# Second half's x and the MLP's h turned by VectorE's 32x32 blocks instead of by TensorE

## The chip, the cores and the metric

One core of one Trainium2 chip runs the whole program. The metric is device time in microseconds (us) of one execution, as the median of several runs; a profiled execution of the same program gives the trace from which the durations below come. The engines are named as the profile names them: PE (TensorE matmuls), PEld (its weight loads), DVE (VectorE), ACT (ScalarE), POOL (GpSimd) and SP (SyncE, which here only issues transfers).

## What is computed

One transformer block over 2048 tokens of 1024 features: a layer norm, an attention of 32 heads with a learned feature map and no quadratic part, a residual, a second layer norm, a ReLU MLP of width 3584, and a second residual.

```python
def _A_ref(x, wqkv, w_phi, wo):            # attention; H = 32, Dh = 32
    q, k, v = ...                          # x @ wqkv, by heads
    pq = einsum("bhsd,hdf->bhsf", q, w_phi);  pk = einsum("bhsd,hdf->bhsf", k, w_phi)
    phi_q = concat([softmax(pq), softmax(-pq)]);  phi_k = concat([softmax(pk), softmax(-pk)])
    kv = einsum("bhsf,bhsd->bhfd", phi_k, v);  z = phi_k summed over s
    o = einsum("bhqf,bhfd->bhqd", phi_q, kv) / (einsum("bhqf,bhf->bhq", phi_q, z) + 1e-6)
    return o @ wo
def _B_ref(x, w1, w2):
    return einsum("bsf,fd->bsd", maximum(einsum("bsd,df->bsf", x, w1), 0), w2)
h  = x + _A_ref(_layernorm(x), A_wqkv, A_w_phi, A_wo)
h2 = h + _B_ref(_layernorm(h), B_w1, B_w2)
```

## The kernel before, in words

Every product of two float32 matrices is made of three matmuls (`mm3`, L181 to L183): each operand is split into a high part and a low part of a shorter type, and high-high, high-low and low-high are added up in PSUM. A group of three such matmuls, each with 512 moving columns, is one **step**. The program is written as a list of items of 8 steps (4 in the MLP), and all other work is hung on steps by hand: `when(step, f, ...)` puts the call `f` into the program behind that step, `do(n, k, f, ...)` behind step k of item n. Each engine runs its own instructions in the order in which they were written, and semaphores do the rest. So a step number is a place in the order, not a time.

The items come in this order. Tokens stand in 16 tiles of 128, in two halves of 8 tiles.

1. For each half: keys and values (`kv_item`, 4 slabs of heads over 8 tiles), then queries (`q_item`, 2 slabs over 8 tiles). The stationary operand is `xT[t]`, the normalized x of a tile with features on the partitions, high and low part.
2. Projection by `wo` (`wo_item`, 4 groups of 4 tiles, 2 halves of the features, 32 tile-halves in all). Between these items PE makes the attention's numerators (`at_num`, L678), in 16 pairs of units, from blocks that DVE has turned (`at_turn`, L664) and POOL has scaled.
3. The MLP up (`up_item`) and down (`down_item`), by a seven-product scheme (Strassen and Winograd's) on halves of tokens and features: the operands 1 to 7 are sums and differences of quarter blocks. The moving operand of an up step is `hT[m]`, the stationary one a piece of w1. Two blocks of 8 tiles follow each other, `b` = 0 and 1.

**Turning x.** `ln_load` loads a tile of x with tokens on the partitions, `ln_norm` (L243, ACT) normalizes it, and `ln_turn` (L250) turns it: 4 PE transposes of 128x128 into one PSUM bank, twice per tile. `split` (L177 and L178) then takes the high part with ACT and the low part with DVE from that bank. The tiles of the second half are turned while the queries' last slab of the first half is projected; their statistics were made much earlier (`scx`).

**Turning h.** `wo_add` (L728) adds x to the projection's bank, `wo_store` writes the sum to `hd[t]` in DRAM. `ln_pair(b, i, stage)` takes two tiles, 4 apart: loads them (stage 0), makes statistics with DVE (1, L220) and POOL (2, L229 to L231), normalizes (3, L243), turns them on PE (4 to 7, L250 and L758) with an ACT copy out of each bank (L252 and L759), and forms the sums that the scheme wants (L760 and L761 on DVE, L766 and L767 on POOL). `ln_store` writes the seven operands to `hs[b, m]`; `h_load` brings them back, `h_high` (L792) and `h_low` (L796) split them into `hT[m]`. Block 0's pairs lie in the wo items, block 1's in the up items of block 0. The table LN2 has the steps of the stages.

**Weights.** `Units` loads weight pieces in the order of their use into 6 raw buffers, splits them (ACT L124, then POOL or DVE L128) into a ring of 10, and runs ahead of PE as far as these allow. All these loads, the loads of x and h and the stores go through SP's one queue, in written order; the attention's blocks (`ed`) go through ACT's queue.

**The end.** `d_load` brings h back from `hd`, `d_add` (L886) adds the MLP's banks to it, `d_store` writes the output.

## Time and profile before

| | us |
|---|---|
| median of 3 runs | 1881.68 (1880.31 to 1882.74) |
| the profiled execution, whole | 1881.49 |
| its span, first to last instruction | 1879.7 |
| PE busy | 1872.6 |
| DVE busy | 1063.6 |
| POOL busy | 976.9 |
| ACT busy | 741.0 |

The span is what the trace shows; the whole execution is 1.8 us longer. Matmuls overlap in the pipeline, so PE's time is read from the distance between the starts of its instructions, not from their durations. In a timeline row the columns are the start in us from the span's start, the duration, engine, line, operation, what is written and read, the shape and the count; in a row of groups there are the busy time, the mean of one in ns and, behind the second bar, the idle time ahead of it and what ended that.

### The profile page before, as it was taken

The numbers are of one execution on the slowest core, as the hardware profiler recorded it, in microseconds if no ns is written. First come the engines' busy times: TensorE is split into PE (matmuls) and PEld (weight loads), VectorE is DVE, ScalarE is ACT, GpSimd is POOL, SyncE is SP. The second block draws the span as 40 slices with busy tenths as digits, with TensorE's granted clock in tenths as the row PEclk, the third lists the DMA queues.
The fourth block names the chain that finished last, engine by engine and source line by source line (L and its number), as shares of the span: only waits on it lengthen the run. The fifth ranks groups of instructions, "written<-read, shape, count | busy, mean of one in ns | idle before, by whom it ended". The sixth has DMA issues, their size and how long they took to land.

```text
span 1879.7 us, 31869 instructions
## 1 busy us (share of the span) xinstructions
PE 1872.6 (100%) x11630; PEld 1540.3 (82%) x11630; DVE 1063.6 (57%) x1714; ACT 741.0 (39%) x1264; POOL 976.9 (52%) x956
## 2 busy tenths in 40 slices
PE   9999999999999999999999999999999999999999
PEld 7888888888888888888888888888888888888887
DVE  7788688677789777455444664444433333343333
ACT  5322244222233122355455554444444444444442
POOL 3778733677745988223343234445444444444443
PEclk9999999999999999999999999999999999999999
DMA  6889875454475567886877997877877677777775
GB/s 214 268 280 312 269 262 180 148 155 141 140 232 190 203 216 237 264 254 209 263 233 241 312 297 248 264 246 259 275 239 216 201 230 239 237 213 220 216 215 177
DMA packets 293036, 433.21 MB, mean 230 GB/s; under 512 B 24208, under 2 KB 150160, under 8 KB 292880
## 3 DMA queue, kind: packets, MB, share of 16 engines
q1 hardware_dynamic: 263712, 390.26, 65.3%
q10 hardware_dynamic: 29168, 40.93, 6.5%
q8 instruction: 91, 1.49, 0.3%
q14 instruction: 65, 0.53, 0.1%
HBM read 293.73 MB, written 137.36 MB: 229 GB/s over the span
## 4 chain that ended last, share of the span: by engine, by line
PE 98%; DVE 1%; ACT 0%; POOL 0%; DMA 0%; issue 0%; SPq 0%; DVEq 0%; POOLq 0%
PE mm L181 25%; PE mm L182 25%; PE mm L183 25%; PE ac L181 4%; PE ac L182 4%; PE ac L183 4%; PE tp L182 2%; PE tp L181 2%; PE tp L183 2%; PE tp L250 1%; PE tp L678 1%; PE ac L491 1%; PE ac L678 1%; PE tp L297 0%; DVE st L220 0%; PE tp L758 0%
## 5 line engine op out<-in xcount | busy, mean ns | idle before, releaser
L128 POOL TENSOR_TENSOR w<-raw,w 128x512 fp32r<-128x512 f32 x353 | 474.6, 1347 | 671.5 <-ACT w L124 638.0
L124 ACT ACTIVATE w<-raw 128x512 fp32r<-128x512 f32 x686 | 409.1, 626 | 491.8 <-PE mm L183 238.9
L128 DVE TENSOR_TENSOR w<-raw,w 128x512 fp32r<-128x512 f32 x333 | 275.0, 827 | 512.9 <-ACT w L124 507.3
L181 PE MATMUL mm<-w,xT 128*128 128x512 f32 x752 | 299.4, 398 | 0.0
L183 PE MATMUL mm<-w,xT 128*128 128x512 f32 x752 | 293.1, 390 | 0.0
L182 PE MATMUL mm<-w,xT 128*128 128x512 f32 x752 | 293.0, 390 | 0.0
L181 PE MATMUL mm<-hT,w 128*128 128x512 f32 x672 | 262.6, 391 | 0.0
L183 PE MATMUL mm<-hT,w 128*128 128x512 f32 x672 | 261.6, 389 | 0.0
L182 PE MATMUL mm<-hT,w 128*128 128x512 f32 x672 | 261.5, 389 | 0.0
L378 POOL TENSOR_TENSOR b<-b 128x256 f32<-128x256 f32 x168 | 129.0, 769 | 85.2 <-DMA b<-in_w_dram 75.4
L181 PEld LDWEIGHTS mm<-w,xT 128*128 128x128 f32 x752 | 141.2, 188 | 31.4 <-issue 2.2
L183 PEld LDWEIGHTS mm<-w,xT 128*128 128x128 f32 x752 | 141.2, 188 | 30.0
L182 PEld LDWEIGHTS mm<-w,xT 128*128 128x128 f32 x752 | 141.3, 188 | 28.5 <-issue 1.0
L181 PE MATMUL mm<-w 128*128 128x512 f32 x392 | 152.5, 389 | 0.0
L182 PE MATMUL mm<-w 128*128 128x512 f32 x392 | 152.5, 389 | 0.0
L183 PE MATMUL mm<-w 128*128 128x512 f32 x392 | 152.5, 389 | 0.0
L183 PEld LDWEIGHTS mm<-hT,w 128*128 128x128 f32 x672 | 126.1, 188 | 26.5
L181 PEld LDWEIGHTS mm<-hT,w 128*128 128x128 f32 x672 | 126.2, 188 | 25.8
L182 PEld LDWEIGHTS mm<-hT,w 128*128 128x128 f32 x672 | 126.2, 188 | 25.7
L480 POOL TENSOR_TENSOR zacc<-zacc,kphi 128x512 f32<-128x512 f32 x60 | 83.8, 1397 | 14.3 <-DVE kphi L472 14.3
L181 PEld LDWEIGHTS mm<-w 128*128 128x128 f32 x392 | 73.6, 188 | 15.3
L182 PEld LDWEIGHTS mm<-w 128*128 128x128 f32 x392 | 73.6, 188 | 15.3
(173 smaller groups left out, 3183.1 us busy)
## 6 DMA issues: line engine op xcount, KB each, us to landing
raw<-t SPq DMA_DIRECT2D x224, 256.0 KB, 4.0
raw<-ad SPq DMA_DIRECT2D x196, 256.0 KB, 3.0
raw<-in_w_dram SPq DMA_DIRECT2D x168, 256.0 KB, 3.2
ad<-c SPq DMA_DIRECT2D x112, 256.0 KB, 4.2
b<-in_w_dram SPq DMA_DIRECT2D x42, 512.0 KB, 5.7
t<-b SPq DMA_DIRECT2D x42, 512.0 KB, 3.6
ad<-s SPq DMA_DIRECT2D x84, 256.0 KB, 4.6
ed<-qe ACTq DMA_DIRECT2D x32, 512.0 KB, 3.9
```

Of the source, the lines that this page charges most:

```text
L124: nc.scalar.activation(w[:, 0, :], raw[1], AF.Copy)
L128: eng.tensor_tensor(out=w[:, 1, :], in0=raw[1], in1=w[:, 0, :].bitcast(F32), op=ALU.subtract)
L181: pe.matmul(ps, a_hi, b_hi, start=first, stop=False, skip_group_check=more)
L182: pe.matmul(ps, a_hi, b_lo, start=False, stop=False, skip_group_check=more)
L183: pe.matmul(ps, a_lo, b_hi, start=False, stop=last, skip_group_check=more)
L250: pe.transpose(pt[:, k, :], xn[:, (4 * j + k) * P:(4 * j + k + 1) * P], ident)
L378: pool.tensor_tensor(out=tsum[j, *out], in0=tsum[j, *a], in1=tsum[j, *b], op=ALU.subtract)
L480: pool.tensor_tensor(out=zacc[s], in0=zacc[s], in1=phi_of[key], op=ALU.add)
L491: pe.matmul(kv_ps[s][g][32 * i:32 * (i + 1), 0:64], vt[:, 32 * h:32 * (h + 1)], phi[:, 64 * h:64 * (h + 1)], start=first, stop=last)
L678: pe.matmul(banks[g][32 * c:32 * (c + 1), r * P:(r + 1) * P], kvL[rows, 4 * q + 2 * sd + h // 4, 32 * (h % 4):32 * (h % 4 + 1)], phT[rows, ...
```

## The change

The second half's x and all of h are no longer turned on PE. A tile is loaded so that a partition holds a quarter of the features of four tokens, one from each group of 32; DVE then turns the tile in place in 32x32 blocks with one instruction, which leaves features on the partitions.

- **x, second half.** `x_load` loads a tile in 4 transfers, one per group of 32 tokens. Partition 32a+j then holds tokens j of the four groups, features 256a to 256a+255. A scale per token therefore differs between the four column groups, so `x_norm` normalizes with 4 ACT instructions of 256 columns (`turn_norm`), from statistics that `x_stats` has brought into that layout by way of DRAM. `x_turn` is the DVE transpose, `x_high` an ACT copy, `x_low_part` two POOL subtractions. The features come out in another order, so the second half's weights for k, v and q are loaded in that order (`rows_of`).
- **h, sums and statistics.** `wo_add` writes the sum into a new tile `xo` (2 buffers; `xh` goes from 5 to 3) with the features regrouped. `wo_stats` makes the statistics from `xo` at once, `wo_power` finishes them on POOL, `wo_keep` stores two numbers per token.
- **h, turning.** `ln_pair` loads each tile in 4 transfers and the statistics in 4 small ones, normalizes with 4 ACT instructions per tile, and turns each tile with one DVE instruction. The ACT copies are gone. The sums are formed as before. The stage table has other steps.
- **The MLP.** `hT[m]` now holds token groups outermost, so that an up matmul reads its 512 moving columns in 16 runs of 32, 128 columns apart (`h_chunk`). It writes PSUM in plain order (`by_token`). `h_load` is one transfer instead of two.
- **The end.** `d_load` fetches h in the regrouped order into a tile `raw`, and the first `d_add` of an output writes a new tile.

```diff
+    def x_load(t):
+        xin["x", t] = (xlp if t % 4 > 1 else lnp).tile([P, D], F32, name="xl" if t % 4 > 1 else "xin")
+        src = x[t * P:(t + 1) * P, :].rearrange("(g j) (a f) -> g a j f", g=4, a=4)
+        for g in range(4):
+            sp.dma_start(xin["x", t][:, 256 * g:256 * (g + 1)], src[g])
+    def turn_norm(dst, src, scale, bias):
+        for g in range(4):
+            c = slice(256 * g, 256 * (g + 1))
+            act.activation(dst[:, c], src[:, c], AF.Identity, bias=bias(g), scale=scale(g))
+    def x_turn(t):
+        xn = xnt["x", t]
+        v.transpose(xn, xn)
+    def x_high(t):
+        (hi, _), xn = x_parts(t)
+        act.activation(hi, xn, AF.Copy)
+    def x_low_part(t, j):
+        (hi, lo), xn = x_parts(t)
+        k = slice(4 * j, 4 * j + 4)
+        pool.tensor_tensor(out=lo[:, k], in0=xn[:, k], in1=f32(hi[:, k]), op=ALU.subtract)
...
+    def rows_of(w, hf, k):
+        return w[k] if hf == 0 else w.rearrange("(a c) p f -> a (c p) f", a=4)[:, 32 * k:32 * (k + 1), :]
...
     def wo_add(t, hf):
-        v.tensor_add(xh[t, hf], wo_ps.pop((t, hf)), xh[t, hf])
+        v.tensor_add(by_row(xo[t, hf]), by_group(wo_ps.pop((t, hf))), by_group(xh.pop((t, hf))))
+    def wo_stats(t, hf):
+        st = hst[t]
+        v.bn_stats(out=st[:, 6 * hf:6 * hf + 6], in_=xo[t, hf])
+        if hf:
+            v.bn_aggr(out=st[:, 12:14], in_=st[:, 0:12].rearrange("p (j c) -> p j c", j=2))
+    def wo_keep(t):
+        sp.dma_start(shd[t // HT, t % 4][:, t % HT // 4, :], hst.pop(t)[:, 14:16])
...
         if stage == 0:
-            for key in keys:
-                ln_load(key, [hd[key[1]]])
+            for t in tiles:
+                hx[t] = lnp.tile([P, D], F32, name="xin")
+                src = hd[t].rearrange("a (g j) r c -> g a j (r c)", g=4)
+                for g in range(4):
+                    sp.dma_start(hx[t][:, 256 * g:256 * (g + 1)], src[g])
...
-        elif stage in (4, 5, 6):
-            ln_turn(keys[stage // 6], stage != 4)
+        elif stage in (4, 5):
+            ht = hx[tiles[stage - 4]]
+            v.transpose(ht, ht)
...
-            mm3(ps, w[:, 0, cols], w[:, 1, cols], hT[m][:, 0, k, :], hT[m][:, 1, k, :],
+            mm3(by_token(ps), w[:, 0, cols], w[:, 1, cols], h_chunk(m, 0, k), h_chunk(m, 1, k),
+    def h_chunk(m, s, k):
+        return hT[m][:, s].rearrange("p i (g k j) -> p k (i g) j", g=4, k=4)[:, k]
...
+            for step, f, *args in ((-11, x_norm), (-6, x_turn), (0, x_high), (2, x_low_part, 0), (4, x_low_part, 1)):
+                when(turn + step, f, t, *args)
...
-        do(max(n - 2, wo_first), -1, wo_load, t, hf)
+        when(8 * n - 4 if n > wo_first + 1 else wo0, wo_load, t, hf)
...
-    LN2 = ((0, 9, 12, 17, 24, 25, 26, 27, 29, 36), (0, 18, 26, 32, 40, 42, 44, 46, 50, 60))
+    LN2 = ((0, 8, 17, 19, 22, 24, 26, 28, 35), (0, 18, 32, 36, 40, 44, 48, 50, 60))
```

The order of instructions moves on PE, and on the queues around the wo items. On PE, in one wo item of the pair of tiles 1 and 5 (`xin` are the two tiles of h, `tp` the PSUM banks of transposes, `oT` the attention's output), before the change:

```order
L183 MATMUL mm_8359<-w_6311,oT_7774 128x512
L250 MATMUL tp_8368<-ident_398,xin_8050 128x128 x4
L181 MATMUL mm_8359<-w_6342,oT_7774 128x512
L182 MATMUL mm_8359<-w_6342,oT_7774 128x512
L183 MATMUL mm_8359<-w_6342,oT_7774 128x512
L250 MATMUL tp_8378<-ident_398,xin_8050 128x128 x4
L181 MATMUL mm_8359<-w_6835,oT_7774 128x512
```

The same item in the changed kernel:

```order
L183 MATMUL mm_8382<-w_6292,oT_7788 128x512
L181 MATMUL mm_8382<-w_6323,oT_7788 128x512
L182 MATMUL mm_8382<-w_6323,oT_7788 128x512
L183 MATMUL mm_8382<-w_6323,oT_7788 128x512
L181 MATMUL mm_8382<-w_6816,oT_7788 128x512
```

The sets of four transposes are gone and the steps follow each other directly; PE's program has 48 rows of this kind fewer, 16 for x and 32 for h, and is otherwise the same.

On SP's queue, at the load of the same pair (`hd` is h in DRAM, `shd` its statistics, `xh` the residual x, `xo` the new sum), before:

```order
L702 DMA xh_8044<-in_x_dram 128x512
L214 DMA xin_8050<-hd1_85 128x1024
L214 DMA xin_8052<-hd5_89 128x1024
L731 DMA hd2_86<-xh_7790 128x512
L702 DMA xh_8169<-in_x_dram 128x512
```

In the changed kernel:

```order
L824 DMA xin_8054<-hd1_85 128x1x256 x4
L824 DMA xin_8059<-hd5_89 128x1x256 x4
L751 DMA xh_8091<-in_x_dram 128x512
L803 DMA hd2_86<-xo_8002 128x4x128
L812 DMA shd0_2_103<-qmx_7620 128x2
L829 DMA st_8197<-shd0_1_102 32x4x4 x4
L751 DMA xh_8227<-in_x_dram 128x512
```

Where two loads stood ahead of the next residual there are now eight, and a store and four loads of statistics stand between that one and the one after it.

More of the change, by code (lines that the diff above doesn't have):

```diff
@@ L209, in ln_load @@
     def ln_load(key, parts):
-        xin[key] = xlp.tile([P, D], F32, name="xl") if key[0] == "x" and key[1] >= HT and key[1] % 4 > 1 else \
-            lnp.tile([P, D], F32, name="xin")
+        xin[key] = lnp.tile([P, D], F32, name="xin")
         n = D // len(parts)
@@ L240, in ln_norm, with ln_turn @@
     def ln_norm(key):
-        sc, src = xst.pop(("s", key[1]) if key[0] == "x" and key[1] >= HT else key), xin.pop(key)
-        xnt[key] = src if key[0] == "h" else fp_ln.tile([P, D], F32, name="xn")
+        sc, src = xst.pop(key), xin.pop(key)
+        xnt[key] = fp_ln.tile([P, D], F32, name="xn")
         act.activation(xnt[key], src, AF.Identity, bias=sc[:, 1:2], scale=sc[:, 0:1])
-    def ln_turn(key, j, dst=None):
+    def ln_turn(key, j, dst):
         xn = xnt[key]
@@ L974 @@
         do(n, 0, x_open, t)
-        for j in range(2):
+        for j in range(2 if t < HT else 0):
             when(stages[4 + j], ln_turn, ("x", t), j, lambda t=t: xT[t])
```

164 lines of the change are left out of this document (109 added, 55 removed).

## The prediction

> **What bounds the kernel now.** I read the page first, then the chain, then the groups of PE, then PE's timeline.
>
> ```profile
> span 1879.7 us, 31869 instructions
> PE 1872.6 (100%) x11630; PEld 1540.3 (82%) x11630; DVE 1063.6 (57%) x1714; ACT 741.0 (39%) x1264; POOL 976.9 (52%) x956
> PE 98%; DVE 1%; ACT 0%; POOL 0%; DMA 0%; issue 0%; SPq 0%; DVEq 0%; POOLq 0%
> ...
> L250 PE MATMUL tp<-ident,xn 128*128 128x128 f32 x120 | 18.1, 273 | 0.5 <-ACT xn L243 0.4
> L250 PE MATMUL tp<-ident,xin 128*128 128x128 f32 x96 | 14.4, 272 | 0.0
> L758 PE MATMUL tp<-ident,xin 128*128 128x128 f32 x32 | 4.8, 272 | 0.0
> ```
>
> PE is busy all through the span and makes 98% of the chain that ended last, so what leaves PE's program leaves the time, as long as nobody else becomes late. The transposes that go are 64 of the 120 on `xn` (8 tiles of 8) and all 96 + 32 on `xin`: 192, in 48 sets of four. Their durations overlap with their neighbours', so the price of a set is read from starts. PE's timeline in the wo items, around the pair of tiles 1 and 5:
>
> ```profile
> 702.09 0.60 PE L250 MATMUL tp<-ident,xin 128*128 128x128 f32 x4
> 702.45 0.47 PE L181 MATMUL mm<-w,oT 128*128 128x512 f32 x1
> ...
> 703.22 0.60 PE L250 MATMUL tp<-ident,xin 128*128 128x128 f32 x4
> ...
> 707.06 0.40 PE L183 MATMUL mm<-w,oT 128*128 128x512 f32 x1
> ...
> 711.83 0.39 PE L183 MATMUL mm<-w,oT 128*128 128x512 f32 x1
> ...
> 311.70 0.60 PE L250 MATMUL tp<-ident,xn 128*128 128x128 f32 x4
> ...
> 312.38 0.39 PE L182 MATMUL mm<-w,xT 128*128 128x512 f32 x1
> ```
>
> From one set to the next with one step between them it is 1.13 us. A matmul without transposes starts 0.227 us after the last (21 between 707.06 and 711.83), a step therefore takes 0.68, and the set costs 1.13 - 0.68 = 0.45 us. At x it is the same: from the start of the set to the step's second matmul 0.68 us, without the set 0.23, difference 0.45.
>
> **The change, part by part.**
>
> *PE.* 48 sets at 0.45 us: 21.6 us, 7.2 of them at x, 7.2 in the wo items, 7.2 in the first block of up items. Nothing is added to PE's program. Added to its work, perhaps: the 2352 up matmuls now read their columns in 16 runs of 32.
>
> ```profile
> L181 PE MATMUL mm<-hT,w 128*128 128x512 f32 x672 | 262.6, 391 | 0.0
> L181 PE MATMUL ac<-hT,w 128*128 128x512 f32 x112 | 43.9, 392 | 0.0
> L678 PE MATMUL tp<-qe,kvL 32*32 32x128 f32 x896 | 24.8, 278 | 0.0
> L297 PE MATMUL mm<-wt,wphi 32*32 32x256 f32 x224 | 10.4, 386 | 0.0
> ```
>
> (672 + 112) x 3 = 2352. No row shows a large matmul with such an operand. The nearest are L678 and L297, whose moving operands are runs of 32 columns: 278 ns for 4 runs against 272 for 128 plain columns (L250), a difference of 6 ns that may belong to the other shape; 386 for 8 runs, below the 391 of 512 plain columns. The bounds are nothing and 6 ns, 2352 x 6 = 14 us; a gain is excluded, since the columns are as many. I take nothing, because L297 with its 8 breaks shows none. [...]
>
> *DVE.* In the x stage it loses 16 subtractions from PSUM and gains 8 transposes of a whole tile, whose price the attention's turning shows.
>
> ```profile
> L664 DVE STREAM_TRANSPOSE qe<-qe 128x1024 f32<-128x1024 f32 x28 | 34.2, 1227 | 12.1 <-POOL qe L658 9.5 <-POOL qe L648 1.7 <-DMA xh<-in_x_dram 1.0
> L178 DVE TENSOR_TENSOR xT<-tp,xT 128x512 fp32r<-128x512 f32 x30 | 20.3, 678 | 6.1 <-ACT xT L177 6.1
> 262.00:315.00 53.00, 53.00 (x266) 43.80 (x265) 46.28 (x71) 29.18 (x40) 15.12 (x17) 1.00 0.69 227
> ```
>
> 16 x 0.678 = 10.8 go, 8 x 1.227 = 9.8 come. DVE has 46.3 us of work in these 53 (third busy column of the windows' row), and will have 45.3 in 53 - 7.2 = 45.8: full. It may fall a us or two behind there; PE waits for it only when four banks are full, three items of 5.4 us later, and the rest of the keys' stage gives the time back. Nothing is charged. If the backlog grew beyond 16 us it would show one for one.
>
> *ACT and POOL at x.* A normalization in four pieces (8 x 4; 0.38 to 0.82 us each by L453 and L237, I take 0.6) and 8 copies of 1024 (1.06 by L792) replace 8 normalizations (1.24) and 16 copies (0.6 by L177); POOL gets 16 subtractions like L128.
>
> ```profile
> L453 ACT ACTIVATE vt<-mm 128x256 f32<-128x256 f32 x64 | 24.5, 382 | 125.0 <-PE mm L183 125.0
> L237 ACT ACTIVATE xn<-xin,sc 128x512 f32<-128x512 f32 x2 | 1.6, 816 | 2.7 <-POOL sc L231 2.7
> L128 POOL TENSOR_TENSOR w<-raw,w 128x512 fp32r<-128x512 f32 x353 | 474.6, 1347 | 671.5 <-ACT w L124 638.0 <-DMA raw<-t 8.9 <-DVE c L822 5.6
> L792 ACT ACTIVATE hT<-hT 128x1024 fp32r<-128x1024 f32 x28 | 29.6, 1056 | 30.5 <-DMA hT<-hs 29.5 <-DMA raw<-in_w_dram 1.1
> L177 ACT ACTIVATE xT<-tp 128x512 fp32r<-128x512 f32 x30 | 17.9, 597 | 33.2 <-PE tp L250 33.1
> L243 ACT ACTIVATE xin<-xin,sc 128x1024 f32<-128x1024 f32 x16 | 19.3, 1236 | 13.5 <-POOL sc L231 12.7 <-DVE oT L695 0.4
> ```
>
> POOL: 16 x 1.35 = 21.6 more beside the 15.1 in that window. ACT has 29.2 + 32 x 0.6 + 8 x 1.06 - 8 x 1.24 - 16 x 0.6 = 37 us of work in 46. Each tile is wanted seven items after it is turned, 38 us, so this hides behind PE; without that cover a tile's chain, some 8 us, would stand in the open once.
>
> *The wo items.* Here the wait that matters is PE's for the attention's turned blocks. DVE's and PE's timelines at two of the 16 pairs:
>
> ```profile
> 631.11 1.19 DVE L664 STREAM_TRANSPOSE qe<-qe 128x1024 f32<-128x1024 f32 x1
> 632.21 0.34 PE L678 MATMUL tp<-qe,kvL 32*32 32x128 f32 x8
> 645.15 0.34 PE L678 MATMUL tp<-qe,kvL 32*32 32x128 f32 x8
> 651.23 1.25 DVE L664 STREAM_TRANSPOSE qe<-qe 128x1024 f32<-128x1024 f32 x1 [0.66 <-POOL qe L658]
> 658.08 0.34 PE L678 MATMUL tp<-qe,kvL 32*32 32x128 f32 x8
> 640.00:660.00 20.00, 20.00 (x329) 16.02 (x327) 14.05 (x26) 1.36 (x5) 17.09 (x24) 1.00 0.61 204
> ```
>
> At 632 the second block of the pair is ready at 632.30 and used by the second half of the numerators, some 0.8 us after 632.21: 0.7 us to spare. At 658 it is ready at 652.48, 5.6 us ahead. Between 632 and 658 no transpose stands on PE, pairs are 12.9 us apart, and the chain still won 5 us. That is the pace which PE will keep through all the wo items, so the loss of the pauses by itself makes nobody late. What is new in this chain: `wo_stats` puts 0.67 us per tile-half on DVE from the first wo item on (L220), where the statistics used to come later, and `wo_power` puts three POOL instructions per tile ahead of step 132, 8 tiles instead of 4.
>
> ```profile
> L220 DVE BATCH_NORM_STATS2 st<-xin 128x6 f32<-128x512 f32 x64 | 40.6, 674 | 4.8 <-DMA xin<-in_x_dram 2.8 <-DMA xin<-hd 2.0
> 657.57 0.22 POOL L229 TENSOR_SCALAR sc<-mv 128x1 f32<-128x1 f32 x1
> ...
> 658.89 0.22 POOL L229 TENSOR_SCALAR sc<-mv 128x1 f32<-128x1 f32 x1
> ```
>
> Up to the pair at 632 DVE gets 4 x 0.674 = 2.7 us more; a tile's three POOL instructions take 1.3 us (658.89 - 657.57), so POOL gets 4 x 1.3 = 5.3 us more before step 132. DVE and POOL are idle for 6 and 3 us of the 20 above. The loss lies between nothing, if the added work falls into waits, and 2.7 + 5.3 = 8.0 us, if none does. I take 2: the DVE part at the pairs with no reserve, most of it; the POOL part falls on pairs with 5 us. DVE's two h transposes per pair (2.5 us) replace nothing on DVE; they come when pairs have that reserve, or after the attention. `wo_add` now also waits for SP to have stored the `xo` of two halves before, written 11 steps (7.5 us) ahead, against 3.6 us to land:
>
> ```profile
> hd<-xh SPq DMA_DIRECT2D x32, 256.0 KB, 3.6
> xh<-in_x_dram SPq DMA_DIRECT2D x32, 256.0 KB, 4.7
> q1 hardware_dynamic: 263712, 390.26, 65.3%
> ```
>
> Behind it on DVE stand the attention's reductions and turns. SP in turn waits with `wo_keep` for POOL, and the next residual loads stand behind that; a residual is asked for 13 steps (9 us) ahead and lands after 4.7, so SP may be held 4 us before DVE notices, and I add nothing.
>
> *Up and down.* Operand 7 of block 0 is the tightest of the up start: split until 823.53, used at 823.87.
>
> ```profile
> 821.18 2.35 DVE L796 TENSOR_TENSOR hT<-hT 128x1024 fp32r<-128x1024 f32 x2
> ...
> 823.87 0.39 PE L181 MATMUL mm<-hT,w 128*128 128x512 f32 x1
> ```
>
> Its load waits for PE to leave the wo items and so moves with PE; it becomes one transfer in long rows instead of two, a us either way, nothing charged. Block 1's transposes and normalizations have 68 steps of up items per pair instead of 40, and I charge nothing. At the end `d_add` is as many instructions as before.
>
> **The sum**, against the profiled execution's 1881.5 us (the median of the runs shown, 1881.68, is the same within their spread): 1881.5 - 21.6 + 2.0 = 1861.9, so 1862.
>
> **The rivals.**
>
> *The attention's chain takes it back.* The 8.0 us above in full: 1881.5 - 21.6 + 8.0 = 1867.9. For it speaks the 0.7 us at 632, against it the 5 us won by 658. It would show as idle PE ahead of L678.
>
> *The new loads crowd few engines.* The sources of `x_load`, of `ln_pair`'s loads and of `rows_of` have four blocks outermost, where every load before has 128 rows. By the queue's row (packets, MB, share of 16 engines), 65.3% of 16 x 1879.7 us for 390 MB, one engine needs 50 us per MB; a pair of h tiles (1.05 MB) takes 53 us, 3.3 on sixteen engines and 13.2 on four. The 9.9 us more would hold what stands behind them on the queue: a transfer of 256 KB would land after 4.7 + 9.9 = 14.6 us. In the wo items that is 5.6 us beyond the 9 that a residual has, and 5 are the chain's reserve: 1 us per pair. In the up items ACT splits a weight 14 steps (9.5 us) after it was asked for, is held 5 us, and the banks bear 2.7 (one item): 2.3 per pair. Four pairs of each make 13 us, if every wait is paid; I take 9, so 1862 + 9 = 1871. No trace here shows such a load. [...]
>
> *The runs slow the up matmuls: slower than before.* If each of the 15 breaks costs the time of two columns (0.227 us / 512 = 0.44 ns each), a matmul takes 13.3 ns more, 2352 of them 31 us: 1862 + 31 = 1893. It decides from (1881.5 - 1861.9) / 2352 = 8.3 ns, 4% of 227. Against it stands L297.
>
> *The transposes were hidden*, and nothing changes, 1881: the starts at 702 speak against it.
>
> **How the numbers follow.** The forecast 0.58, the chain 0.12, the crowded engines 0.18, the runs 0.10, hidden 0.02. The range runs from 1857.5 (no loss, 1859.9, less the runs' spread and 0.03 us in a set's price) to 1877, which holds the first two rivals unless both come in full (0.03 of the second's 0.18); left out are these, the runs, the hidden case and 0.03 below, 0.18 in all. This kernel's measurement tells 0.2% from no change, 3.8 us. Faster by more: 0.58 + 0.12 + 0.15 = 0.85; within: 0.03 + 0.02 = 0.05; slower: 0.10.
>
> **What would show it.** Right: up matmuls 0.227 us apart, no L250-like rows after the first half's tiles, PE's stages shorter by 7.2 us each, idle PE ahead of the numerators below 3 us. Wrong: starts of up matmuls more than 8 ns further apart; `hd` loads that land 10 us or later; ACT waiting for loads in the up items.

## The result, and the profile after

The changed kernel takes 2008.79 us (median of 5 runs, 2008.51 to 2014.04) against 1880.31 (1880.19 to 1882.74) for the kernel before on the same chip: a ratio of 1.0687, 95% interval 1.0671 to 1.0702. The forecast was 1862 with a range up to 1877; the time lies far outside it, on the other side.

The page of the changed kernel: the span, the busy times, the engines' shares of the chain, and the first row of the up matmuls. The chain could be followed back only to 885 us, so its shares say nothing of the stages before that.

```profile
span 2007.0 us, 31636 instructions
PE 1911.9 (95%) x11438; PEld 1539.6 (77%) x11438; DVE 1075.5 (54%) x1722; ACT 739.5 (37%) x1296; POOL 997.0 (50%) x972
PE 53%; DMA 1%; DVE 1%; SPq 0%; issue 0%; POOL 0%; DVEq 0%; POOLq 0%
...
L181 PE MATMUL mm<-hT,w 128*128 128x512 f32 x672 | 270.5, 402 | 4.5 <-ACT hT L878 2.7
```

PE has 192 instructions fewer and yet 39 us more of busy time, and now it also stands still: 95% busy where it was 100%. The up matmuls are longer, 402 ns where the row showed 391. PE's timeline in the up items of block 1, where nothing waits, gives the distance of their starts:

```profile
1299.61 0.40 PE L181 MATMUL mm<-hT,w 128*128 128x512 f32 x1
1299.84 0.40 PE L182 MATMUL mm<-hT,w 128*128 128x512 f32 x1
1300.08 0.40 PE L183 MATMUL mm<-hT,w 128*128 128x512 f32 x1
1300.31 0.40 PE L181 MATMUL mm<-hT,w 128*128 128x512 f32 x1
```

0.23 to 0.24 us here, 237 ns at the median of all 2352, 227 before. For the rest I cut the span of a profiled execution at PE's starts into stages: the first 40 items, the 8 items in which the second half's x is turned (x stage), the second half's remaining keys and queries, the wo items, the up items of block 0 and of block 1, and the rest. In us:

| kernel | first 40 | x stage | keys, queries | wo | up 0 | up 1 | rest |
|---|---|---|---|---|---|---|---|
| before | 260.1 | 50.3 | 285.7 | 206.1 | 274.1 | 266.3 | 537.2 |
| after | 260.0 | 59.3 | 345.2 | 238.0 | 289.2 | 278.1 | 537.2 |

The loss is 60 us in the second half's keys and queries, a stage that the prediction did not price at all, 32 in the wo items, 9 in the x stage, and 12 to 15 in each block of up items. What PE waited for from the x stage to the end of the queries (us in all, times, longest; before, PE had no such row in that window):

```profile
PE mm L181 <- ACT w L124: 13.9, 1, 13.9
PE mm L182 <- POOL w L128: 12.2, 6, 7.2
PE mm L181 <- DVE qe L612: 10.1, 3, 7.3
PE tp L567 <- POOL zacc L529: 8.9, 2, 5.4
PE mm L182 <- DVE w L128: 6.5, 3, 5.1
```

In the first, second and last row PE lacks the weights' halves, from all three engines that make them; in the other two it waits for work of the attention on DVE and POOL. One step further back stands POOL's wait for `b`, the loads of pieces of w1 and w2 whose sums POOL forms beside the attention. In the kernel before, from 310 to 665 us (us in all, times, longest):

```profile
POOL b L378 <- DMA b<-in_w_dram: 33.9, 10, 5.0
```

In the changed kernel, in the same window:

```profile
POOL b L427 <- DMA b<-in_w_dram: 79.2, 12, 13.4
```

These loads are not touched by the change, and POOL waits up to 13 us for one. They share SP's queue with loads that are new. How few engines the new ones use is seen from 347 to 351 us, where nearly all that moves is the second half's weights, which SP issues one behind the other (PE, PEld, DVE, ACT, POOL busy, then the granted clock, the DMA share and GB/s):

```profile
347.00:351.00 4.00, 4.00 (x20) 3.30 (x19) 0.00 (x0) 0.08 (x1) 1.37 (x2) 1.00 0.27 95
```

A share of 0.27 is 4.3 of the 16 DMA engines, and at 95 GB/s 128 KB take 1.38 us; the mean over the whole span is 216 GB/s.

Of the prediction's own signs of error the first is there: starts of up matmuls 10 ns further apart, where 8 was the bound. So is the third: in the up items ACT waits 14.5 us for loads of weights, 1.1 before. The second, `hd` loads that land late, can't be read, since this trace gives no landing for them.

### The profile page after: what moved, and what is told of

Same layout as the page of the kernel before. It is cut to its first block, busy times and chain, and to the rows that moved or that the text cites. A ratio compares the mean times of both kernels' runs of the same rounds, so it can differ in the third digit from the quotient of the medians.

```text
span 2007.0 us, 31636 instructions
## 1 busy us (share of the span) xinstructions
PE 1911.9 (95%) x11438; PEld 1539.6 (77%) x11438; DVE 1075.5 (54%) x1722; ACT 739.5 (37%) x1296; POOL 997.0 (50%) x972
## 4 chain that ended last, share of the span: by engine, by line
PE 53%; DMA 1%; DVE 1%; SPq 0%; issue 0%; POOL 0%; DVEq 0%; POOLq 0%
PE mm L183 12%; PE mm L181 12%; PE mm L182 12%; PE ac L183 3%; PE ac L181 3%; PE ac L182 3%; PE tp L182 2%; PE tp L181 2%; PE tp L183 2%; DMA hd<-xo 1%; DMA hT<-hs 0%; DVE hT L882 0%; SPq L396 0%; DVE xo L791 0%; DVE w L128 0%
## 5 line engine op out<-in xcount | busy, mean ns | idle before, releaser
L181 PE MATMUL mm<-w,xT 128*128 128x512 f32 x752 | 304.7, 405 | 24.1 <-ACT w L124 13.9
L182 PE MATMUL mm<-w,xT 128*128 128x512 f32 x752 | 300.6, 400 | 18.9 <-POOL w L128 12.2
L183 PE MATMUL mm<-w,xT 128*128 128x512 f32 x752 | 298.4, 397 | 0.0
L181 PE MATMUL mm<-hT,w 128*128 128x512 f32 x672 | 270.5, 402 | 4.5 <-ACT hT L878 2.7
L182 PE MATMUL mm<-hT,w 128*128 128x512 f32 x672 | 269.7, 401 | 3.8 <-DVE hT L882 3.8
L183 PE MATMUL mm<-hT,w 128*128 128x512 f32 x672 | 270.1, 402 | 0.0
L181 PEld LDWEIGHTS mm<-w,xT 128*128 128x128 f32 x752 | 144.8, 193 | 59.7 <-ACT w L124 14.3
L182 PEld LDWEIGHTS mm<-w,xT 128*128 128x128 f32 x752 | 144.8, 193 | 55.0 <-POOL w L128 16.7
L183 PEld LDWEIGHTS mm<-w,xT 128*128 128x128 f32 x752 | 144.7, 192 | 30.5
L513 ACT ACTIVATE ke<-ke 128x512 f32<-128x512 f32 x64 | 40.4, 631 | 144.2 <-DVE ke L509 144.2
L182 PEld LDWEIGHTS mm<-w 128*128 128x128 f32 x392 | 73.6, 188 | 15.3
```

Source lines behind the costliest of these rows:

```text
L181: pe.matmul(ps, a_hi, b_hi, start=first, stop=False, skip_group_check=more)
L182: pe.matmul(ps, a_hi, b_lo, start=False, stop=False, skip_group_check=more)
L183: pe.matmul(ps, a_lo, b_hi, start=False, stop=last, skip_group_check=more)
L513: act.activation(e_of[key], e_of[key], AF.Exp)
```

## The experiments

All ratios are to the kernel before on the same chip, with 95% intervals. There is no kernel 6 or 7. A stage's time is that of the one profiled execution, which can lie a few us beside the median. Kernels 2 to 5, 8, 9, 11, 12, 15 and 16 start from the changed kernel and let columns or feature chunks meet that belong to different tokens or features; kernels 10, 14 and 17 to 20 keep them together.

**1. The runs alone.** The kernel before, with only the operand of the up items read in 16 runs of 32 (tokens in another order):

```diff
...
-            mm3(ps, w[:, 0, cols], w[:, 1, cols], hT[m][:, 0, k, :], hT[m][:, 1, k, :],
+            mm3(by_token(ps), w[:, 0, cols], w[:, 1, cols], h_chunk(m, 0, k), h_chunk(m, 1, k),
```

> The kernel before, whose up matmuls alone now read their 512 columns in 16 runs of 32, 128 columns apart, from the same tiles (so tokens and features are mixed up in the MLP). Theory 'runs' (a broken moving operand costs time by itself): the up matmuls start 0.237 us apart as in the changed kernel, 10 ns more, 2352 x 10 ns = 23.5 us, so 1904 us. Theory 'company' (the 10 ns come from what else runs in the changed kernel): 0.227 us apart and 1880 us.

1903.41 us, ratio 1.0118 (1.0103 to 1.0133). Nothing else moved: up 0 takes 285.5, up 1 278.1 us, all other stages are those of before within 1.6 us. The runs cost 1903.41 - 1880.73 (the kernel before, beside it) = 22.7 us, 9.6 ns for each of 2352 matmuls.

**2 to 4. Plain operands, wide loads, both.** In 3, each load with four blocks outermost gets 32 or 128 rows outermost: x and h in 4 transfers by feature quarter, onto 32 partitions each, instead of by token group, the weights in their plain order. In 2, the operand is read plainly. 4 is both.

```diff
-        src = x[t * P:(t + 1) * P, :].rearrange("(g j) (a f) -> g a j f", g=4, a=4)
-        for g in range(4):
-            sp.dma_start(xin["x", t][:, 256 * g:256 * (g + 1)], src[g])
+        src = x[t * P:(t + 1) * P, :].rearrange("(g j) (a f) -> a j g f", g=4, a=4)
+        for a in range(4):
+            sp.dma_start(xin["x", t][32 * a:32 * (a + 1)].rearrange("p (g f) -> p g f", g=4), src[a])
...
-        return w[k] if hf == 0 else w.rearrange("(a c) p f -> a (c p) f", a=4)[:, 32 * k:32 * (k + 1), :]
+        return w[k]
...
-        return hT[m][:, s].rearrange("p i (g k j) -> p k (i g) j", g=4, k=4)[:, k]
+        return by_token(hT[m][:, s, k, :])
```

> The changed kernel, whose up matmuls read 512 plain columns again (the operand's columns stand in another order, so tokens and features are mixed up in the MLP). Theory 'runs': 0.227 us apart in both blocks of up items, 2009 - 23.5 = 1985 us, and the stretch from 262 to 950 us as it was. Theory 'company': no change, 2009 us.

> The changed kernel with every load made of pieces whose outermost count is 32 or 128: x and h are loaded in 4 transfers by feature quarter onto 32 partitions each, instead of by token group onto 128, and the second half's weights for k, v and q are loaded in plain order (so their features no longer match those of x). Theory 'four engines' (176 transfers with an outermost count of 4 run on 4 of the 16 DMA engines, and PE's stalls and the low clock behind them come from that): the trace shows 16 completions per transfer, no gap of PE above 1 us after the first 62 us but a few, and 1880 - 21.6 + 23.5 + 2 = 1884 us (1880 to 1892). Theory 'work' (the new instructions and waits on DVE, POOL and SP make the stalls): 1985 us or more.

> Both edits: wide loads and plain columns, with the parts of the computation changed that these two change. If the two causes are all there is, what is left is the transposes' 21.6 us and my 2 us of lost reserve: 1861 us (1858 to 1866). If theory 'work' holds, 1960 us or more.

| kernel | us | ratio | x stage | keys, queries | wo | up 0 | up 1 |
|---|---|---|---|---|---|---|---|
| 2 | 1990.46 | 1.0581 (1.0563 to 1.0598) | 62.5 | 342.5 | 234.5 | 285.5 | 266.4 |
| 3 | 1917.58 | 1.0194 (1.0179 to 1.0209) | 43.5 | 301.3 | 213.0 | 285.5 | 278.1 |
| 4 | 1892.87 | 1.0066 (1.0049 to 1.0083) | 43.5 | 302.1 | 211.5 | 270.8 | 266.3 |

The loads cost 2008.8 - 1917.6 = 91 us; the runs, on top of wide loads, 24.7. In 2, plain operands alone win 18.3 us and not 23.5: up 1 is 11.7 us shorter, up 0 only 3.7. That a four-block load runs on four engines only agrees with the smallest packets: the trace of the kernel before has 23,185 of 4 bytes for 1449 transfers, 16 for each and one over. The changed kernel's 1546 transfers leave 22,625; by 16 each it would be 24,736, and with four from each of the 176 transfers of x, h and weights it is 22,624. The third kernel has 24,737, the fifth (below; 96 such transfers left) 23,585. That each such packet stands for one engine is a reading of these counts beside the 4.3 engines of 347 to 351 us. In the third kernel POOL's wait for `b` is back near its old size (same window):

```profile
POOL b L427 <- DMA b<-in_w_dram: 39.0, 11, 5.3
```

So 4 still lies 32 us above its expectation: something more is at work, in three stages (16 us in the keys and queries, 13 in the wo items, 4 in up 0).

**5. Which of the loads.** Only the second half's weights are wide; x and h keep their four blocks (`return w[k]` in the changed kernel).

> The changed kernel with the second half's weights loaded as before, 128 rows outermost (the product of x then meets weights of other features: its value is not the reference's). Theory, four engines crowded: wide loads in all three places gained 91 us, 25 of them in the wo items, where only h's loads are concerned, 4 in the up items, and 60 in the x stage and the second half's keys and queries, where the loads of x (8 x 0.5 MB) and of these weights (80 of 128 KB on average, 14.7 MB in all) share the blame. If the weights carry it by their bytes, 45 of the 60 go: about 1964. If the loads of x carry it (they come first and hold the queue), 5 to 15 go and the time stays near 2000.

1949.74 us (one run), 59 less than the changed kernel: x stage 45.3, keys and queries 305.4, POOL's wait for `b` 33.0 us. The 80 weight loads (64 of 128 KB, 16 of 256 KB; 12.6 MB and not the 14.7 of the expectation) carry two thirds of the 91 us. The loads of x, which the expectation's second branch blamed, carry nearly nothing: 45.3 for 43.5 and 305.4 for 301.3. The wo items and up 0 keep 236.9 and 286.6; 24 and 1 us go there only with h's loads.

**8. x in place.** The x stage of 4 is as short as forecast, but work falls behind in it, and the keys and queries pay. It is seen on ACT, which normalizes a tile every 7.25 us where PE takes 5.4 for an item. Its timeline, normalizations alone (at the end the idle time before and what ended it):

```profile
279.04 2.08 ACT L237 ACTIVATE xn<-xl,srx 128x256 f32<-128x256 f32 x4 [2.65 <-POOL xT L260]
286.29 2.08 ACT L237 ACTIVATE xn<-xin,srx 128x256 f32<-128x256 f32 x4 [2.66 <-POOL xT L260]
293.53 2.08 ACT L237 ACTIVATE xn<-xin,srx 128x256 f32<-128x256 f32 x4 [2.66 <-POOL xT L260]
```

`xn` has two buffers: the normalization of tile t+2 waits until POOL has subtracted tile t, which waits for ACT's high part of t, which waits for the normalization of t, turned by DVE. In the eighth kernel the tile is normalized where it was loaded:

```diff
-        src = xin.pop(("x", t))
-        xnt["x", t] = xn = fp_ln.tile([P, D], F32, name="xn")
+        xn = src = xnt["x", t] = xin.pop(("x", t))
...
-            load_ = turn - 88 + 8 * (t - HT) if t < HT + 4 else turn - 36
+            load_ = turn - 88 + 8 * (t - HT) if t < HT + 4 else turn - 27
```

> The fourth kernel (all loads wide, operands plain: 1892.9) with x normalized in place in the tile that its load filled, not into one of two xn buffers; a load that takes a tile over is asked for 9 steps later. Theory, a loop of two buffers: normalization of tile t+2 waits for POOL's subtraction of tile t, 7.2 us a tile on ACT against 5.4 on PE, and what ACT does late are the weights' copies of the next stage; in place the normalizations run ahead, the second half's keys and queries take 286 instead of 302 us, and the time is 1877. Rival, ACT and POOL simply have too much work there: the stage keeps 298 or more, the time 1889 or more.

1876.96 us, ratio 0.9979 (0.9970 to 0.9988). Keys and queries take 284.8 us, and PE waits for nothing there. In the fourth kernel PE's longest wait from 262 to 600 us was this:

```profile
PE mm L181 <- ACT w L124: 10.0, 1, 10.0
```

**9. A third buffer for the sum.** DVE's sum waits up to 6 us for the store of `xo`; 3 buffers for `xo` and 2 for `xh` instead of 2 and 3, on the fourth kernel.

> The fourth kernel with three buffers for xo and two for xh instead of two and three (the same memory). Theory, the sum waits for its buffer's store: DVE's 13.9 us of waiting for hd's store at the sum goes, the attention's chain keeps its reserve, the wo items take 200 instead of 211.5 us, and the time is 1882. Rival, the added statistics, turns and normalizations hold DVE, POOL and ACT by themselves (8 us were the upper bound in the prediction) or the loads of h hold the queue: the wo items keep 208 or more, the time 1890 or more.

1894.26 us, ratio 1.0076 (1.0054 to 1.0098); the wo items take 215.8 us (in the profiled execution, with 1901.18 the longest of the four). Nothing is won, but the run doesn't settle the theory: DVE's 10.9 us of waiting for the store in the wo items of 4 are gone, and with one buffer less for `xh` DVE waits 8.2 us for the residual instead. The twelfth kernel (below) settles it: it has two buffers, DVE waits for the store (587 to 787 us), and the wo items still take 199.2 us, so this wait is not on PE's path.

```profile
DVE xo L790 <- DMA hd<-xo: 20.4, 5, 9.1
```

Another wait stands higher in the ninth kernel's wo items (615 to 840 us), ACT's for the statistics:

```profile
ACT xin L237 <- DMA st<-shd: 39.6, 4, 13.4
```

**12, 11, 15, 16. What of the statistics.** All on the eighth kernel, whose wo items take 212.6 us where 206.1 - 7.2 = 198.9 was forecast. Its waits from 615 to 830 us:

```profile
DVE xo L790 <- DMA hd<-xo: 21.1, 6, 6.1
...
ACT xin L237 <- DMA st<-shd: 19.4, 2, 10.1
POOL qmx L806 <- DVE qmx L796: 18.9, 10, 6.1
```

POOL's first instruction for a tile's statistics (L806) waits for DVE's, with the attention's products queued behind. 12 leaves h's statistics out (wo_stats, wo_power, wo_keep; h is scaled by numbers of x). 15 leaves out POOL's part alone (the store then keeps mean and variance, by which h is scaled). 11 puts POOL's part 6 steps later. 16 is 11 with the pairs of h later, so that ACT finds its statistics there.

```diff
# 12
-        when(8 * n + 10 + late_, wo_stats, t, hf)
-            when(8 * n + 12, wo_power, t)
-            when(8 * n + 16, wo_keep, t)
# 15
-            when(8 * n + 12, wo_power, t)
# 11
-            when(8 * n + 12, wo_power, t)
-            when(8 * n + 16, wo_keep, t)
+            when(8 * n + 18, wo_power, t)
+            when(8 * n + 22, wo_keep, t)
# 16, on 11
-            when(wo0 + 64 + 40 * i + LN2[0][stage], ln_pair, 0, i, stage)
+            when(wo0 + 72 + 38 * i + LN2[0][stage], ln_pair, 0, i, stage)
```

> The eighth kernel without h's statistics: DVE's, POOL's and the 16 stores of them are left out, and h is normalized with numbers of x's statistics. Theory, the statistics in the attention's chain (DVE 23.9 us, POOL 22.9 us and 18.9 of waiting): the wo items take 200 to 203 us, the up start 268, and the time is 1860 to 1866. Rival, the 12 loads per pair on SP's queue and ACT's eight normalizations per pair hold the chain: the wo items keep 208 or more, 1872 or more.

> The eighth kernel (wide loads, plain operands, x in place: 1877.0, wo items 212.6 us against 198.9 = 206.1 - 7.2 that the transposes promise) with POOL's three instructions for a tile's statistics 6 steps (4 us) later and their store 6 steps later. Theory, POOL held in order: these instructions wait for DVE's statistics, 18.9 us in 10 waits, and the attention's products for the denominators and the scaling are queued behind them; later they find the statistics done, the wo items take 203 to 206 us, and the time is 1868 to 1871. Rival, POOL's or DVE's added work itself, or the loads of h: the wo items keep 210 or more, the time 1874 or more.

> The eighth kernel without POOL's three instructions for a tile's statistics: DVE takes them as before and SP keeps its mean and variance, by which h is then scaled (not the reference's value). Without all of the statistics it was 1859.7, with them 1877.0, with POOL's part 4 us later 1870.6. Theory, POOL is the price, by its waits for DVE and by 23 us of work on an engine that the attention's chain fills: the wo items take 200 to 202 us, the time is 1861 to 1864. Rival, DVE's 24 us are the price: the wo items keep 207 or more, the time 1869 or more. Both: between.

> The eleventh kernel (POOL's statistics 4 us later: 1870.6) with each pair of h tiles loaded, normalized and turned 8, 6, 4 and 2 steps later. Theory, ACT held in order: a normalization that waits for its statistics (10.4 us once between 640 and 750) holds the attention's loads, which ACT issues, and POOL waits for these (8.2 us); later pairs find their numbers there, the wo items take 204 instead of 208.7 us, the time is 1865 to 1867. Rival, the 8 loads of a pair take SP 7 us to issue and stretch ACT's own issues wherever they stand: nothing changes, 1869 to 1872.

| kernel | us | ratio | wo | up 0 |
|---|---|---|---|---|
| 8 | 1876.96 | 0.9979 (0.9970 to 0.9988) | 212.6 | 272.6 |
| 12, no statistics | 1859.67 | 0.9884 (0.9868 to 0.9900) | 199.2 | 268.7 |
| 15, without POOL's part | 1864.97 | 0.9916 (0.9901 to 0.9931) | 200.1 | 270.6 |
| 11, POOL's part later | 1870.59 | 0.9947 (0.9929 to 0.9965) | 208.7 | 269.2 |
| 16, and later pairs | 1876.33 | 0.9976 (0.9967 to 0.9985) | 208.5 | 279.0 |

The statistics cost 1877.0 - 1859.7 = 17.3 us, POOL's part 12.0 of them; 4 us of delay in the order wins back 6.4. The other 5 are left for DVE's 24 us and the stores. In 11, POOL's own wait for DVE is nearly gone (590 to 760 us):

```profile
POOL qmx L806 <- DVE qmx L796: 3.2, 2, 1.6
```

So about half of POOL's price was won back by the later place; that the rest is its work is likely, but not shown. 16 misses: the wo items stay, and up 0 is 10 us longer, since its first operands come late: PE stands idle for 6.5 us there where 11 has 2.3, and the clock granted on average over its span is 0.995 where 11's is 0.998 (last section). ACT's waits at the normalizations only went from 26 to 20 us there, so whether they have a price isn't settled by it.

With the statistics out as well, the kernel stands at 1859.7, where the forecast's mechanism has it: wo items 199.2 for 198.9, x stage 43.5 for 43.1. But it does without work that the kernel before does.

**13. The length of a run.** The kernel before, its seven operands read in runs of different lengths.

```diff
+    RUN = {1: 32, 5: 64, 6: 128, 2: 256, 7: 16, 3: 8, 4: 512}
+    def h_runs(m, s, k):
+        h = hT[m][:, s].rearrange("p i n -> p (i n)")
+        return h.rearrange("p (n k j) -> p k n j", k=4, j=RUN[m])[:, k]
...
```

> The kernel before, in which the up items of the seven operands read their 512 columns in runs of 32, 64, 128, 256, 16, 8 and 512 columns (in the order of the operands 1, 5, 6, 2, 7, 3, 4; the columns belong to other tokens, so its product is not the reference's). Read from the starts within the items. Theory, a price for each run: 10 ns for 16 runs of 32 (measured), so 5 for 8 of 64, 2.5 for 4 of 128, 20 for 32 of 16, 40 for 64 of 8, and up items of 336 matmuls each add 1.7 + 3.4 + 0.8 + 6.7 + 13.4: about 1907. Rival, a price only for runs below some length: 128 and 256 at 227 ns (128 was, in the tenth kernel), a step at 64 or 32, and the short ones far dearer.

1893.07 us (one run). Mean distance of starts within an item, in ns (median over the 14 pairs of items):

| columns in a run | 512 | 256 | 128 | 64 | 32 | 16 | 8 |
|---|---|---|---|---|---|---|---|
| ns | 229.4 | 226.7 | 226.7 | 227.7 | 236.6 | 242.1 | 231.7 |

PE's timeline in runs of 256 (1218), and in runs of 16 (1223):

```profile
1218.06 0.39 PE L182 MATMUL ac<-hT,w 128*128 128x512 f32 x1
1218.29 0.39 PE L183 MATMUL ac<-hT,w 128*128 128x512 f32 x1
1218.51 0.39 PE L181 MATMUL ac<-hT,w 128*128 128x512 f32 x1
...
1222.98 0.41 PE L182 MATMUL mm<-hT,w 128*128 128x512 f32 x1
1223.22 0.41 PE L183 MATMUL mm<-hT,w 128*128 128x512 f32 x1
1223.47 0.41 PE L181 MATMUL mm<-hT,w 128*128 128x512 f32 x1
```

There is no price per run: from 64 columns (256 bytes) on 1 ns at most, at 32 columns 10 ns, at 16 15, and at 8 less again. Each length stands on one operand alone; why it is so isn't known. (The operand of 512 comes last before the next group; its fastest items stand at 226.6 too.)

**10. Short rows instead.** x and h loaded in runs of 128 bytes, so that chunks have the weights' own order, with both the eighth's and the ninth's edits; the operand is 4 runs of 128 columns.

```diff
+        src = x[t * P:(t + 1) * P, :].rearrange("(g j) (k a i) -> a j k g i", g=4, k=NK, a=4)
```

> Both mendings at once, and with the reference's output: x and h are loaded by feature quarter onto 32 partitions in runs of 128 bytes, so that the chunks come in the weights' own order and the weights are loaded as before; an operand of the up items is then 4 runs of 128 columns. Theory: 1892.9 less 16 for the loop, less 10 for xo: 1867. If 4 runs cost a matmul what 16 do (10 ns) it is 1890; if a quarter of that, 1873. If the short rows make the loads slow (8 x 4096 rows in x, 16 x 4096 in h), PE waits in the x stage and in the wo items, and the time is over 1890 with plain operands' cadence.

1906.88 us, ratio 1.0138 (1.0121 to 1.0155). The up matmuls stand 227 ns apart. But SP needs longer to issue such a load: 0.68 us at the median of the 16 into `xl`, 0.43 in the eighth kernel, and now and then far more. On its timeline, two transfers of a tile in the tenth kernel, of which one takes 3.52 us:

```profile
221.89 4.28 SPq L222 DMA_DIRECT2D xl<-in_x_dram  x2
```

Four of them in the eighth:

```profile
237.37 3.51 SPq L222 DMA_DIRECT2D xl<-in_x_dram  x4
```

Again `b`, behind them in the queue, is late at POOL (tenth kernel, 250 to 320 us; 7.9 us in the eighth):

```profile
POOL b L425 <- DMA b<-in_w_dram: 17.7, 3, 10.2
```

x stage 49.8, keys and queries 294.2: the price of the short rows, as the expectation's last branch had it. The wo items (219.2) and up 0 (277.6) lose too; the ninth's edit, which is in it, had lost 4 and 5 us there.

**14, 17, 20, 19. All of it mended, nothing left out.** In 14, x is normalized when its statistics are made and kept in DRAM by feature quarter; the load has rows of 1 KB and the chunks their natural order. DVE turns h into another tile, chunk by chunk (operand: 4 runs of 128). POOL's part is 11's. 17 puts the early normalization 6 steps later and takes 16's pairs; 20 takes only the former; 19 is 20 with one POOL instruction per tile instead of three; DVE and ACT take over the rest.

```diff
+        act.activation(xn.rearrange("p (a k i) -> p k a i", a=4, k=NK),
+                       src.rearrange("p (k a i) -> p k a i", a=4, k=NK), AF.Identity, ...)
+        sp.dma_start(xd[t].rearrange("a p f -> p a f"), ...)
...
+            dst_, src_ = dst.rearrange("p (k g j) -> p g k j", k=8, g=4), src.rearrange("p (g k j) -> p g k j", k=8, g=4)
+            v.transpose(dst_, src_)
```

> All mendings in one kernel that gives the reference's output: x is normalized when its statistics are taken and kept by feature quarter in another memory of the kernel, so that its load is 4 wide transfers in rows of 1 KB, its chunks have the weights' own order, and ACT's four pieces per tile leave the x stage; DVE turns h into another tile, chunk by chunk, so that an operand is 4 runs of 128 columns; POOL's statistics come later. Theory: x stage 43.5, keys and queries 285, wo items 203 to 206, up start 268, up matmuls 227 ns apart: 1865 to 1870. If what is left in the wo items is the loads of h or the turning, 1874 to 1878. If the early normalizations disturb the first 40 items, the first stage is longer than 260 us and the time higher by that.

> The fourteenth kernel (the reference's output, 1879.4) with x's early normalization 6 steps later, so that ACT doesn't wait there for POOL's statistics (14.4 us) with the weights' copies behind it, and with the later pairs of the sixteenth. Theory: the first 40 items take 259 to 260 instead of 265.2 us, the wo items 204 to 206 instead of 210.4: 1867 to 1870. If ACT's wait was harmless and the early normalizations or their stores cost by themselves, the first 40 items keep 264 or more and the time is 1873 or more.

> The fourteenth kernel with only x's early normalization 6 steps later (the pairs in their old places). Theory: the first 40 items take 262 instead of 265.2 us and the rest stays: 1874 to 1877. If the late pairs of the seventeenth kernel were not what cost its up start 7 us, it stays at 1880.

> The fourteenth kernel (the reference's output, 1879.4: first 40 items 265.2 us, wo items 210.4) with x's early normalization 6 steps later, and with one of POOL's three instructions per tile of h left: DVE adds the epsilon right behind its statistics, POOL takes the power, and ACT works out the biases at the normalization. Theory, POOL is most of the statistics' price (12 of 17 us): the first 40 items take 262, the wo items 203 to 206 us, the up start 269: 1865 to 1869. If any instruction of POOL that waits for DVE costs the same, whatever its length, the wo items keep 209 and the time is 1872 or more.

| kernel | us | ratio | first 40 | wo | up 0 |
|---|---|---|---|---|---|
| 14 | 1879.42 | 0.9989 (0.9978 to 1.0001) | 265.2 | 210.4 | 269.4 |
| 17 | 1881.63 | 1.0003 (0.9992 to 1.0014) | 261.8 | 209.0 | 276.9 |
| 20 | 1877.24 | 0.9978 (0.9968 to 0.9989) | 261.4 | 210.2 | 272.1 |
| 19 | 1876.92 | 0.9977 (0.9969 to 0.9986) | 261.2 | 211.0 | 270.6 |

All four have an x stage of 43.5, keys and queries of 284.8 and up matmuls 227 ns apart. 20 and 19 are 0.2% faster than the kernel before, and all four far faster than the changed one. 14 and 17 miss what was expected of them: in 14 the first 40 items and the wo items are too long, in 17 up 0 as well, which 20, without the later pairs, has back. ACT's early wait for POOL goes with the 6 steps, and 4 us with it. In the fourteenth kernel, 100 to 265 us:

```profile
ACT xn L227 <- POOL sc L274: 14.4, 5, 6.1
```

In the twentieth:

```profile
ACT xn L227 <- POOL sc L274: 1.2, 1, 1.2
```

19 misses in the wo items: with a third of POOL's instructions they take as long as in 20. Its own waits show why it doesn't settle the question: ACT, which now works out the biases, waits there for the statistics, and the attention's loads stand behind (590 to 760 us):

```profile
ACT st L828 <- DMA st<-shd: 13.4, 2, 9.4
POOL ez L663 <- DMA qe<-ed: 13.3, 5, 4.9
```

So how much of POOL's price is the length of its work, and why the wo items of these kernels stay 11 us above 198.9, is open; the fifteenth kernel only shows that the most goes with POOL's part.

**18. Four transfers per weight.** The changed kernel's weights in its own order, each in 4 transfers of 32 rows; with 14's turning, 8's place for x, and POOL's part once for a pair after the load.

```diff
+        rows = w.rearrange("(a c) p f -> a (c p) f", a=4)[:, 32 * k:32 * (k + 1), :]
+        for a in range(4):
+            sp.dma_start(t[32 * a:32 * (a + 1)], rows[a])
```

> All causes mended, and the reference's output: x and h loaded in 4 transfers onto 32 partitions each; the second half's weights in 4 transfers of 32 rows in the order that x's turned features have; x normalized in place; h turned into another tile, so that an operand is 4 runs of 128 columns; of h's statistics only mean and variance are stored with the tile, and POOL works out scale and bias once for a pair, after they were loaded again. Theory, nothing else was at work: first 40 items 259, x stage 43.5, keys and queries 285, wo items 200 to 202, up start 268 to 270, 227 ns up matmuls: 1861 to 1866, below the kernel before. If 320 transfers for weights instead of 80 are too many for SP's queue, keys and queries take over 290; if POOL's wait for the loaded statistics holds the attention's chain, the wo items take over 205.

1949.96 us, ratio 1.0367 (1.0353 to 1.0381): keys and queries 347.1, wo 215.4. The wo items miss their 202 too. Each transfer lands early (1.8 us, median). In the keys and queries this kernel differs from the eighth (284.8) by the weights' transfers alone, so they cost 62 us there. What grows is SP's time: its issues in this stage add up to 137 us, against 49 in the eighth. Four of them, for one half of a weight, take 2 us (SP's timeline):

```profile
378.40 2.17 SPq L405 DMA_DIRECT2D raw<-wpk  x4
380.62 1.81 SPq L405 DMA_DIRECT2D raw<-in_wv_dram  x4
```

On POOL's timeline `b`, from the same queue, is waited for once more (92 us in this stage, 35 in the eighth):

```profile
353.44 0.73 POOL L431 TENSOR_TENSOR b<-b 128x256 f32<-128x256 f32 x1 [20.72 <-DMA b<-in_w_dram]
```

## Why the prediction was wrong, step by step

From the changed kernel down, each step on top of the one before: wide loads 91.2 us, plain operands 24.7, x in place 15.9, no statistics 17.3; 2008.8 - 149.1 = 1859.7. Against before that is -21.6 + 149.1, and the forecast had -21.6 + 2.0. The term that failed most is one that the sum does not have, the new loads: at nothing in the forecast, 9 us in their rival, 91 measured.

- **The PE term held.** 48 sets of 0.45 us were 21.6 us; the twelfth kernel lies 1881.25 - 1859.67 = 21.6 below the kernel before. By stage 6.8, 6.9 and 5.4 for three times 7.2, 19.1 in all; the first 40 items and the keys and queries, which it leaves alone, differ by 1.5 and 0.9. So the transposes are worth about what was forecast, but that the whole agrees to 0.1 us is luck.
- **"I take nothing, because L297 with its 8 breaks shows none."** This step failed: 10 ns, not 0, and outside the bounds of 0 to 6 that the two rows gave. L297 and L678 are small matmuls of 32x32, and their durations were compared, which overlap (eight of L678, 278 ns each, take 0.34 us together at 632.21); the price was read from the distance of starts of matmuls of 512 columns, 237 for 227 ns. The third rival ("13.3 ns, 31 us") had the place and nearly the size, but not the reason: a price per break would be seen at 64 and 128 columns, and it is not (227.7 and 226.7 ns).
- **The rival of few engines had the mechanism, and failed in its price.** Its chance was 0.18. "Four pairs of each make 13 us, if every wait is paid": it priced the pairs of h, 8 transfers each, and passed over `rows_of`, which it names in its first sentence. The 80 weight loads alone carry 59 us. Of h's part it had 4 in the wo items and 9 in the up items; measured are 24 and 1. That four blocks outermost mean four engines was its assumption, which no row of the kernel before shows; the changed kernel shows a DMA share of 0.27 from 347 to 351 us, 4.3 of 16 engines, and its 22,625 packets agree. The size comes by the order of the queues: a late load of `b` holds POOL, POOL's split of a weight comes late, and SP, which waits for that buffer, holds the next weights. SP's waits for it ahead of the weights' loads in the keys and queries, in the changed kernel (319 to 665 us) and in the eighth (303 to 588):

```profile
SPq L383 <- POOL w L128: 28.3, 6, 20.9
...
SPq L382 <- POOL w L128: 15.5, 8, 3.2
```

Not separated is how much of the 60 us comes from the four engines' rate and how much from SP, whose issues in this stage add up to 103 us where before they were 47. The eighteenth kernel, whose transfers have 32 rows each, loses as much without four-block loads, so SP's time may be enough for it.

- **"ACT has 37 us of work in 46 ... so this hides behind PE."** Failed, 16 us. The work fits, as the eighth kernel shows; with two buffers it isn't allowed to run ahead. The cover named, seven items, was not there, since a tile's chain of 7.25 us repeats itself through `xn`.
- **"The loss lies between nothing and 8.0 us. I take 2."** Failed, 17 us (13 of them in the wo items). The upper end counted the added work; POOL's instructions waited 18.9 us for DVE, with the attention's products behind them, and 12.0 of the 17 go with POOL's part. A bound by work is none for an instruction that can wait in an ordered queue.
- **Steps that held at nothing.** DVE full in the x stage: 43.5 us with all of it in place. The `xo` store: DVE waits 20.4 us, and the wo items take 199.2 (twelfth kernel). Operand 7 at the up start: up 0 at 268.7 for 266.9, below 2 us. The first rival, the chain, is the place of the fourth failure, at twice its price.

## What to carry to other kernels

Price an edit by every transfer whose outermost count it changes, the weights too (176 transfers of four blocks cost 91 us here), and look in the trace at the share of busy DMA engines while these transfers run (0.27 here, 4.3 of 16) and at the 4-byte packets per transfer (16 before, four in these). Add up the time that the issuing engine spends on its transfers: here 47 us before, 103 and 137 in the two kernels that lose 60 in that stage. When work is moved to engines that have room, look for the smallest number of buffers in its chain and for instructions that wait ahead of others' work: both cost what shares of busy time don't show (here 15.9 us with two buffers of `xn`, and 6.4 won back when POOL's waiting instructions came 4 us later). A layout that leaves an operand in runs is tried alone on the chip before the rest is built on it; the runs of 32 cost 22.7 us alone.

## What was not expected of the hardware

After a gap PE lost more here than the gap. In the changed kernel the x stage and the keys and queries lost 68.5 us, PE's waits there add up to some 53. Its windows (PE, PEld, DVE, ACT, POOL busy, then the granted clock, the DMA share and GB/s):

```profile
275.00:290.00 15.00, 14.87 (x67) 12.02 (x65) 8.36 (x11) 6.19 (x9) 4.75 (x4) 1.00 0.43 153
...
305.00:320.00 15.00, 8.08 (x27) 6.28 (x28) 7.12 (x10) 8.16 (x12) 4.61 (x5) 0.77 0.60 196
320.00:340.00 20.00, 5.56 (x15) 3.55 (x13) 12.85 (x19) 12.45 (x20) 11.73 (x12) 0.62 0.26 90
340.00:370.00 30.00, 29.18 (x120) 23.64 (x119) 22.33 (x43) 7.05 (x13) 13.04 (x13) 0.91 0.42 141
```

The clock is 1.00 ahead of the long waits, 0.62 in them and still 0.91 in the 30 us behind, in which PE is 97% busy. In PE's starts it is seen directly: behind the wait of 13.9 us they lie 0.43 us apart up to 345.2, but for one more short wait, and 0.23 after that.

```profile
338.49 0.63 PE L181 MATMUL mm<-w,xT 128*128 128x512 f32 x1
338.91 0.63 PE L182 MATMUL mm<-w,xT 128*128 128x512 f32 x1
...
346.39 0.39 PE L181 MATMUL mm<-w,xT 128*128 128x512 f32 x1
346.62 0.39 PE L182 MATMUL mm<-w,xT 128*128 128x512 f32 x1
```

An estimate from windows of 1 us each, PE's busy time times what the clock lacks of 1.00, gives 17 us lost in these two stages, beside 54 us of idle PE: 71 of the 76 us by which they exceed the kernel before without its transposes. In the wo items it is 10.5 and 28.4, 38.9 of 39.1. So here a wait of PE is paid with about a third on top. The other surprises are the runs' price, which sets in between 64 and 32 columns (227.7 and 236.6 ns) and falls again at 8 (231.7, after 242.1 at 16), and that the issue of a four-block load held SP longer. The second half's 32 loads from `in_wv_dram`, 128 KB each, take it 0.54 to 3.05 us in the changed kernel, 1.28 at the median; before, 0.42 to 1.03 and 0.43. One row of each:

```profile
344.35 2.12 SPq L384 DMA_DIRECT2D raw<-in_wv_dram  x1
...
310.68 0.43 SPq L339 DMA_DIRECT2D raw<-in_wv_dram  x1
```

What lengthens the issue isn't shown. The loads of the queries' weights, twice as large and of four blocks as well, take 0.53 us at the median; and 1.28 us is near the 1.38 that 128 KB take at 95 GB/s, so SP may be waiting for the four engines.
